# Attention feeding a mixture of experts: fewer filling products, one write of the last unit's rows, an earlier table, another wait on SyncE, two splits moved

## The chip, the cores and the metric

The kernel runs on one core of a Trainium2 chip. The time is that of the device in microseconds (us), measured over whole executions. The engines are called by the profile's names: PE (TensorE, matrix products), PEld (its weight loads), DVE (VectorE), ACT (ScalarE), POOL (GpSimd) and SP (SyncE, which only issues transfers).

## The reference

The kernel computes attention and gives its output, without leaving the chip, to a layer of experts:

```python
# q, k, v: (4 batches, 12 heads, 448 rows, 64)
scores = cap * np.tanh(scale * (q @ k.T) / cap)        # cap = 30
attn = softmax(scores)
x = (attn @ v) -> rows of 4 * 448 = 1792 tokens, 768 wide
logits = (x / |x|) @ (emb / |emb|).T / tau             # 8 experts
expert = argmax(logits); gate = softmax(logits)[expert]
for e in range(8):                                     # w1[e]: 768 x 1024, w2[e]: 1024 x 768
    h = np.maximum(x[expert == e] @ w1[e], 0)
    out[expert == e] = gate * (h @ w2[e])
```

Which expert a token goes to is known only when its attention is done. How many tokens each expert has is data, so the kernel gathers its tiles of 128 rows by a table of row numbers that it computes itself.

## The kernel before

**Precision.** The products of the experts use two half-precision parts of each factor (high and low), as three products: high by high, low by high, high by low. So a weight that has come from memory is split: ACT writes the high part (L238) and DVE the low part (L239). The rows of a tile, x_tile, are transposed on PE (L226), and split in the same way into xh (ACT, L229) and xl (DVE, L230).

**Start.** PE first runs filling products (`warm`, L293) on constants; one tiny product (`cap_t`, L292) that spreads the value cap over all lanes stands in the middle of them, after the eighth of sixteen. Then the attention's scores begin. The tables of expert embeddings are normalised on DVE, transposed on PE, and multiplied into v (`embed_v`), so that the attention gives the logits as extra columns of x.

**Attention.** `attention_bounded` runs 12 units of two head pairs each, in 7 steps: scores on PE, tanh (L839) and exp (L843) on ACT, and four steps later the product with v (L878). `take` divides the sums of a head pair by their denominators on DVE (L891 to L905) and puts them into the buffer xsb, and `write_rows` (L463) has SP write these columns to x_dram in memory: once after each of a unit's two takes, 144 columns wide. For the last batch each is a pair of transfers, for the row blocks "a" and "c". A take of the last unit writes the buffer from which the earlier write reads.

**First expert.** The expert with the most tokens in the first batches is chosen early; its weights are loaded and split during the attention. Its first tile's up products follow the last unit (`do_up`); between them the squares of x (L443), the one-hot choice of experts (`oh_all`, L485) and the ranks of the last batch (L509) are worked out.

**Table and second tile.** The second tile of the first expert runs through `tile_body`: two halves of up products (`up`, L248, 72 products each in 6 calls), `relu` (ACT L259, DVE L260 `hl`), then eight calls of `down` (L687); between the sixth and seventh it transposes the next tile's x. `hook(n)` runs what a table lists for place n: hooks1 (L1333) puts `slots` at 0, and at 12, which is behind both halves and their relus, `fill_table` (L1263), `positions` and `start_loads2` (L1313). `fill_table` multiplies 16 times on PE (`tabp`, L1266), writes the table of row numbers on DVE (L1267), has POOL gather the first tile by it (L207: indices to idx_in, then an indirect transfer into xg), scales the gathered rows into x_tile (`scale_x`: POOL first copies the gate out of xg, L213, then the expert's number to pos_l, then multiplies, L216) and gathers the next tile into the same xg. `start_loads2` has SP read pos_l, which comes behind the gather on POOL, and then issue the loads of the second expert's weights that are still missing: three of w1 (w1r, L1316) and four of w2 (w2r). So these loads stay behind the first gather. The splits of the first three w1 loads stand at places 12, 13 and 14.

**Chain.** `chain(0)` runs the remaining tiles of the first expert. Its first tile splits the other seven loads of the second expert: `step` takes them from a list, with the counts of `pace`: FIRST0 = (1, 1, 1) means one ahead of each half of the ups, and one ahead of each of the first six downs while any are left. With 2 + 6 places all seven are split before the transposes of the next tile (and before `along_transpose`, L1404 to L1407, which does the same for the tails of other experts). The orders of PE, ACT, DVE and POOL are those in which the code is written (`manual_schedule`).

Of the kernel before, what the change touches and what calls it, by code (L numbers as in the profile page):

```python
# [33 lines left out]
I32 = mybir.dt.int32  # L34
# [42 lines left out]

WARM, EARLY = 4, 16

# [5 lines left out]

FIRST, FIRST0 = (4, 4, 1), (1, 1, 1)

# [8 lines left out]
def attention_moe(ctx: ExitStack, tc: tile.TileContext, q, k, v, cap, emb, tau, w1, w2, qk_pairs, v_pairs, vt_pairs, out):  # L96
# [114 lines left out]

    def scale_x(then=None):
        nc.gpsimd.tensor_copy(gate_s, xg[:, GATE : GATE + 1])  # L213
        if then:
            then()
        nc.gpsimd.tensor_tensor(  # L216
            x_tile.rearrange("p (h d) -> p h d", d=DH), heads(xg[:, :SCALE]),
            xg[:, SCALE : SCALE + 1].unsqueeze(2).to_broadcast([P, H, DH]), op=ALU.mult,
        )

    def transpose_x():
# [65 lines left out]
    with tc.tile_pool(name="ps_w", bufs=1, space=PSUM) as ps_w:  # L287
        warm = ps_w.tile([P, 512], F32, name="warm")
        for n in range(EARLY):
            if n == EARLY // 2:  # L290
                t = ps_t.tile([P, 512], F32, tag="t", name="cap_t")
                nc.tensor.matmul(t[:, 0:1], ones_1, cap_b[0:1], start=True, stop=True)  # L292
            nc.tensor.matmul(warm, ones16, a_all[:, 0:4, :], start=True, stop=True)  # L293
# [26 lines left out]
    with ExitStack() as actx:  # L320
# [339 lines left out]
        def tile_body(p, idx, nxt, todo=(), pace=FIRST, hooks=(), hidden=None, first=False, holds=True):  # L660
# [13 lines left out]
            def step(n):  # L674
                for _ in range(min(n, len(todo))):
                    f, *a = todo.pop(0)
                    f(*a)
# [27 lines left out]
            for f in range(6):  # L705
                hook(2 * DC + f)
                step(pace[2])
                down(f)
# [94 lines left out]
        def attention_bounded(apool, ps_s):  # L803
# [145 lines left out]
            with tc.manual_schedule():  # L949
# [21 lines left out]
                for g0 in range(0, last_step + LAG, 2):  # L971
# [8 lines left out]
                    for j in (g0 - LAG, g0 + 1 - LAG):  # L980
                        if j < 0:
                            continue
                        values(j)
                        i, u = divmod(j, STEPS)
                        if u == REST:
                            take(2 * i)
                            behind += 1.1 if i < NH - 3 else 1.4
                            b, n = divmod(i, NP // 2)
                            write_rows(b, 4 * n * HW, (4 * n + 2) * HW, "ac" if b == last else "a")
                        if u == STEPS - 1:  # L990
                            take(2 * i + 1)
                            behind += 1.1 if i < NH - 3 else 1.4
                            b, n = divmod(i, NP // 2)
                            if b < last:
                                odd_heads(b, n)
                            write_rows(b, (4 * n + 2) * HW, 4 * (n + 1) * HW, "ac" if b == last else "a")
                            if n == NP // 2 - 1 and b < last:
                                after(b)
# [198 lines left out]
    pos_i = work.tile([1, 2, E], I32, name="pos_i")  # L1197
    pos_l = work.tile([1, 1], I32, name="pos_l")
    table = work.tile([P, NTAB], I32, name="table")
# [63 lines left out]
    def fill_table(start):  # L1263
# [4 lines left out]
        gather(col(start))  # L1268
        scale_x(lambda: nc.gpsimd.tensor_copy(pos_l, pos_e[:, 1:2]))
        gather(col(start + 1))  # L1270
# [42 lines left out]
    def start_loads2():  # L1313
        e = nc.values_load(pos_l, engines=(ET.SP,), min_val=0, max_val=E - 1)
        for i in range(SOON, N1):
            nc.sync.dma_start(raw1[i], w1_part(e, i))  # L1316
        for f in range(N2):
            nc.sync.dma_start(raw2[f], w2_part(e, f))

    ends = {}  # L1320

    def load_ends(p):
# [14 lines left out]
        ],  # L1337
        12: [lambda: fill_table(start), positions, start_loads2],
        13: [lambda: along_gather()],
# [464 lines left out]
```

## Time and profile before

| What | us |
|---|---|
| median of three timed runs | 463.24 (463.09 to 463.65) |
| profiled execution, whole | 460.33 |
| its span (first to last instruction) | 458.7 |
| PE busy | 427.9 (93%) |
| ACT busy | 280.7 (61%) |
| DVE busy | 258.0 (56%) |
| POOL busy | 103.5 (23%) |
| PE clock granted over the span, mean | 0.981 of full |

The span is 1.63 shorter than the profiled execution's time, and that execution is 2.9 shorter than the timed median. A share of busy time is an average over all stages. In the rows below, a line gives the start in us from the span's begin, the length in us of the group of instructions that follow one another, the engine, the source line and the operation; in brackets stands how long the engine was idle before it, and what ended that. PEclk is the clock that PE was granted: 1.00 is 2.4 GHz, 0.50 is 1.2 GHz.

### The profile page before, as it was taken

The numbers are of one execution on the slowest core, as the hardware profiler recorded it, in microseconds if no ns is written. First come the engines' busy times: TensorE is split into PE (matmuls) and PEld (weight loads), VectorE is DVE, ScalarE is ACT, GpSimd is POOL, SyncE is SP. The second block draws the span as 40 slices with busy tenths as digits, with TensorE's granted clock in tenths as the row PEclk, the third lists the DMA queues.
The fourth block names the chain that finished last, engine by engine and source line by source line (L and its number), as shares of the span: only waits on it lengthen the run. The fifth ranks groups of instructions, "written<-read, shape, count | busy, mean of one in ns | idle before, by whom it ended". The sixth has DMA issues, their size and how long they took to land. (4 is left out here: it accounts for less than half of the span.)

```text
span 458.7 us, 16438 instructions
## 1 busy us (share of the span) xinstructions
PE 427.9 (93%) x6981; PEld 345.9 (75%) x6982; DVE 258.0 (56%) x679; ACT 280.7 (61%) x341; POOL 103.5 (23%) x177
## 2 busy tenths in 40 slices
PE   8999999999999998897979999999999999999971
PEld 3787888887887887584868968878869788687750
DVE  5254268588987897984591128521117711287841
ACT  4998999999998993524651237512228612477840
POOL 4000000100010302115691322312312313214430
PEclk9899999999999999998989999999999999999996
DMA  6754766866687672045982229912207832199110
GB/s 247 233 147 131 230 183 215 270 185 246 209 249 243 175 231 66 6 174 168 364 350 74 74 93 400 400 74 74 73 5 271 281 156 74 24 322 305 62 42 11
DMA packets 37260, 81.80 MB, mean 178 GB/s; under 512 B 8319, under 2 KB 18203, under 8 KB 37156
## 3 DMA queue, kind: packets, MB, share of 16 engines
q1 hardware_dynamic: 33794, 67.35, 43.2%
q0 software_dynamic: 2720, 13.05, 8.8%
q8 instruction: 63, 1.03, 0.9%
q14 instruction: 41, 0.34, 0.2%
q10 hardware_dynamic: 642, 0.03, 0.1%
HBM read 68.37 MB, written 12.21 MB: 176 GB/s over the span
## 5 line engine op out<-in xcount | busy, mean ns | idle before, releaser
L878 PEld LDWEIGHTS v<-vb,prob 128*64 128x64 f32 (+1 forms) x2688 | 79.8, 137 | 17.4 <-issue 16.1
L878 PE MATMUL v<-vb,prob 128*64 128x73 f32 (+1 forms) x2688 | 87.1, 230 | 1.6 <-issue 1.6
L839 ACT ACTIVATE prob<-s,icap 128x896 f32<-128x896 f32 x84 | 80.2, 998 | 11.2 <-PE s L829 9.8
L843 ACT ACTIVATE prob<-prob,cap_b 128x1792 f32<-128x1792 f32 (+1 forms) x47 | 76.8, 1633 | 1.5
L248 PEld LDWEIGHTS <-h 128*128 128x128 f16 x960 | 74.8, 99 | 3.1 <-ACTq L1180 1.3
L248 PE MATMUL h<-xl,h 128*128 128x128 f16 x432 | 74.2, 221 | 1.7 <-DVE xl L230 1.7
L248 PE MATMUL h<-xh,h 128*128 128x128 f16 x432 | 74.2, 221 | 1.6 <-ACTq L1180 0.9
L248 PE MATMUL h<-xh,l 128*128 128x128 f16 x432 | 74.1, 221 | 0.0
L260 DVE SCALAR_TENSOR_TENSOR hl<-h,hh 128x512 f16<-128x512 f32 (+1 forms) x19 | 12.9, 677 | 69.1 <-ACT hh L259 69.1
L248 PEld LDWEIGHTS <-l 128*128 128x128 f16 x480 | 47.4, 99 | 1.9 <-issue 1.9
L259 ACT ACTIVATE hh<-h 128x512 f16<-128x512 f32 (+1 forms) x19 | 11.1, 586 | 59.0 <-PE h L248 55.6
L239 DVE SCALAR_TENSOR_TENSOR l<-w1r,by_pos,h 128x1024 f16<-128x1024 f32 x30 | 37.1, 1281 | 16.3 <-ACT h L238 16.3
L687 PEld LDWEIGHTS <-hh 128*128 128x128 f16 x320 | 31.1, 99 | 19.2 <-issue 1.1
L1449 PE MATMUL h<-xh,h 128*128 128x160 f16 x192 | 39.9, 233 | 3.0 <-ACT room L314 1.9
L229 ACT CAST xh<-xt 128x384 f16<-128x384 f32 x30 | 13.0, 480 | 44.8 <-PE xt L226 44.8
L1449 PE MATMUL h<-xh,l 128*128 128x160 f16 x192 | 39.9, 233 | 0.0
L1449 PE MATMUL h<-xl,h 128*128 128x160 f16 x192 | 39.9, 233 | 0.0
L687 PE MATMUL v<-h,hl 128*128 128x384 f16 x160 | 39.4, 329 | 0.5 <-DVE hl L260 0.5
L687 PE MATMUL v<-h,hh 128*128 128x384 f16 x160 | 39.5, 329 | 0.4 <-DVE left L1299 0.4
L687 PE MATMUL v<-l,hh 128*128 128x384 f16 x160 | 39.6, 329 | 0.1
L239 DVE SCALAR_TENSOR_TENSOR l<-w2r,by_pos,h 128x1536 f16<-128x1536 f32 x20 | 35.5, 1814 | 3.8 <-ACT h L238 3.8
L230 DVE TENSOR_TENSOR xl<-xt,xh 128x384 f16<-128x384 f32 x30 | 15.4, 552 | 39.4 <-ACT xh L229 39.2
(310 smaller groups left out, 814.5 us busy)
## 6 DMA issues: line engine op xcount, KB each, us to landing
w1r<-in_moe_w_dram SPq DMA_DIRECT2D x30, 512.0 KB, 6.3
w2r<-in_moe_w_dram SPq DMA_DIRECT2D x20, 768.0 KB, 7.6
qkb<-in_qk_pairs_dram SPq DMA_DIRECT2D x11, 896.0 KB, 6.2
vb<-in_v_pairs_dram SPq DMA_DIRECT2D x12, 511.0 KB, 5.5
x_dram<-xsb SPq DMA_DIRECT2D x27, 216.0 KB, 3.9
vt<-in_vt_pairs_dram SPq DMA_DIRECT2D x12, 448.0 KB, 4.7
ring<-in_moe_w_dram SPq DMA_DIRECT2D x6, 512.0 KB, 5.7
ring<-in_moe_w_dram SPq DMA_DIRECT2D x5, 384.0 KB, 4.6
```

What stands on the lines that cost most here:

```text
L229: nc.scalar.copy(hi, t)
L230: nc.vector.tensor_tensor(lo, t, hi, op=ALU.subtract)
L239: nc.vector.scalar_tensor_tensor(out=lo, in0=raw, scalar=scale, in1=hi, op0=ALU.mult, op1=ALU.subtract, accum_out=acc)
L248: nc.tensor.matmul(hp[:, f, :], l[j][:, c], x[:, j, :P], start=j == 0 and f == 0 and n == 0, stop=j == DC - 1 and f == 3 and n == 2, skip_ ...
L259: nc.scalar.activation(hh, hp, AF.Relu)
L260: nc.vector.scalar_tensor_tensor(out=hl, in0=hp, scalar=0.0, in1=hh, op0=ALU.max, op1=ALU.subtract, accum_out=acc[:, h : h + 1])
L687: nc.tensor.matmul(y, hidden[h][l][:, c, :], w2p[p % 2][w][f // 2][:, f % 2, m * 384 : (m + 1) * 384], start=f == 0 and n == 0, stop=f == ...
L839: nc.scalar.activation(o, sp[:, :, :S], AF.Tanh, scale=icap)
L843: nc.scalar.activation(o, o, AF.Exp, scale=cap_b)
L878: nc.tensor.matmul(psum_v[2 * i + n][h * DH : (h + 1) * DH, m * VW : (m + 1) * VW], pt[rows, s, c : c + DH], vb[rows, k, s, :], start=m == ...
L1449: nc.tensor.matmul(o, w1p[p % 2][l][j][:, c], x[:, j, :], start=j == 0 and f == fs[0] and m == 0, stop=j == DC - 1 and f == fs[-1] and m == 2,
```

## The change

1. EARLY falls from 16 to 8 filling products, and cap_t stands after the third.
2. FIRST and FIRST0 get other last numbers, and `tile_body` takes one split ahead of each of the first pace[2] downs instead of pace[2] ahead of each of six. For FIRST0 = (1, 1, 3) five splits stand ahead of the transposes, and two come at the end of the tile.
3. The last unit writes its rows once, 288 columns after its second take, instead of 144 after each take.
4. `fill_table` moves from place 12 to 11, which is ahead of the last call of `up` and of the second relu.
5. pos_l and its copy go. SP issues a transfer of one element, `landed<-xg`, which waits for the gather, and then the loads by the register that it already has. The next gather overwrites xg and so waits for `landed`.
6. `scale_x` multiplies first and copies the gate after it, everywhere.

```diff
-WARM, EARLY = 4, 16
+WARM, EARLY = 4, 8
-FIRST, FIRST0 = (4, 4, 1), (1, 1, 1)
+FIRST, FIRST0 = (4, 4, 6), (1, 1, 3)
...
-    def scale_x(then=None):
-        nc.gpsimd.tensor_copy(gate_s, xg[:, GATE : GATE + 1])
-        if then:
-            then()
+    def scale_x():
         nc.gpsimd.tensor_tensor(
             x_tile.rearrange("p (h d) -> p h d", d=DH), heads(xg[:, :SCALE]),
             xg[:, SCALE : SCALE + 1].unsqueeze(2).to_broadcast([P, H, DH]), op=ALU.mult,
         )
+        nc.gpsimd.tensor_copy(gate_s, xg[:, GATE : GATE + 1])
...
         for n in range(EARLY):
-            if n == EARLY // 2:
+            if n == 3:
...
             for f in range(6):
                 hook(2 * DC + f)
-                step(pace[2])
+                step(f < pace[2])
                 down(f)
...
-                            write_rows(b, 4 * n * HW, (4 * n + 2) * HW, "ac" if b == last else "a")
+                            if i < NH - 1:
+                                write_rows(b, 4 * n * HW, (4 * n + 2) * HW, "ac" if b == last else "a")
...
-                            write_rows(b, (4 * n + 2) * HW, 4 * (n + 1) * HW, "ac" if b == last else "a")
+                            c0 = (4 * n + 2 * (i < NH - 1)) * HW
+                            write_rows(b, c0, 4 * (n + 1) * HW, "ac" if b == last else "a")
...
         gather(col(start))
-        scale_x(lambda: nc.gpsimd.tensor_copy(pos_l, pos_e[:, 1:2]))
+        nc.sync.dma_start(landed, xg[0:1, 0:1])
+        scale_x()
         gather(col(start + 1))
...
     def start_loads2():
-        e = nc.values_load(pos_l, engines=(ET.SP,), min_val=0, max_val=E - 1)
         for i in range(SOON, N1):
-            nc.sync.dma_start(raw1[i], w1_part(e, i))
+            load1(1, i)
         for f in range(N2):
-            nc.sync.dma_start(raw2[f], w2_part(e, f))
+            load2(1, f)
...
-        12: [lambda: fill_table(start), positions, start_loads2],
+        11: [lambda: fill_table(start)],
+        12: [positions, start_loads2],
```

How the instructions of two engines stand at the places where they move (the numbers behind a name are those of buffers). DVE in the second tile of the first expert, from the comparison that `slots` ends with (bm) to the first row of `positions` (val); hl0 and hl1 are the low parts of the two relus. Before:

```order
L1255 TENSOR_TENSOR bm_4981<-iota_t_80,slot_4968 128x640
L260 SCALAR_TENSOR_TENSOR hl0_5056,acc_4854<-h0_4852,hh0_5055 128x512
L260 SCALAR_TENSOR_TENSOR hl1_5132,acc_4854<-h1_4853,hh1_5131 128x512
L702 TENSOR_TENSOR sums_132<-sums_132,acc_4854 128x2
L1267 TENSOR_SCALAR table_4820<-tabp_5137 128x40
L1274 COPY val_4816<-scale_w_104 128x16
```

The same stretch of DVE in the changed kernel (line numbers are those of its code):

```order
L1255 TENSOR_TENSOR bm_4971<-iota_t_80,slot_4958 128x640
L258 SCALAR_TENSOR_TENSOR hl0_5046,acc_4844<-h0_4842,hh0_5045 128x512
L1267 TENSOR_SCALAR table_4810<-tabp_5109 128x40
L258 SCALAR_TENSOR_TENSOR hl1_5151,acc_4844<-h1_4843,hh1_5150 128x512
L700 TENSOR_TENSOR sums_132<-sums_132,acc_4844 128x2
L1275 COPY val_4806<-scale_w_104 128x16
```

The table's row has moved ahead of the second relu's low part. The second place is ACT at the end of chain(0)'s first tile: h2 with a number and w2r are the high part and the raw form of a piece of w2, xt are the transposed rows of the next tile, along_h those of the tails. Before:

```order
L238 ACTIVATE h210_4798<-w2r0_4812,by_pos_4817 128x1536
L238 ACTIVATE h211_4799<-w2r1_4813,by_pos_4817 128x1536
L238 ACTIVATE h212_4800<-w2r2_4814,by_pos_4817 128x1536
L238 ACTIVATE h213_4801<-w2r3_4815,by_pos_4817 128x1536
L229 CAST xh_136<-xt0_5553 128x3x128
L229 CAST xh_136<-xt1_5559 128x3x128
L231 COPY gates2_138<-gates2_138 128x1
L1406 CAST along_h_4824<-s0_5585 128x384
L1406 CAST along_h_4824<-h2_5591 128x384
L1414 COPY xh_136<-along_h_4824 128x6x32
```

The same stretch of ACT in the changed kernel:

```order
L236 ACTIVATE h210_4788<-w2r0_4802,by_pos_4807 128x1536
L236 ACTIVATE h211_4789<-w2r1_4803,by_pos_4807 128x1536
L227 CAST xh_136<-xt0_5529 128x3x128
L227 CAST xh_136<-xt1_5535 128x3x128
L229 COPY gates2_138<-gates2_138 128x1
L1407 CAST along_h_4814<-s0_5561 128x384
L1407 CAST along_h_4814<-h2_5567 128x384
L1415 COPY xh_136<-along_h_4814 128x6x32
L236 ACTIVATE h212_4790<-w2r2_4804,by_pos_4807 128x1536
L236 ACTIVATE h213_4791<-w2r3_4805,by_pos_4807 128x1536
```

The last two splits of w2 now stand behind the casts of the transposed rows; DVE's halves of them move in the same way.

## Rows read from the trace of the kernel before

**Rows 1.** Windows by stage: us, busy (count) of PE PEld DVE ACT POOL, PEclk, DMA, GB/s
```profile
14.80:18.10 3.30, 3.30 (x40) 2.62 (x38) 1.33 (x2) 3.23 (x5) 0.13 (x1) 0.50 0.58 134
213.00:216.10 3.10, 3.10 (x12) 2.17 (x13) 1.11 (x2) 1.05 (x3) 2.43 (x7) 0.50 0.92 318
237.10:240.00 2.90, 2.90 (x28) 2.90 (x28) 2.76 (x4) 0.53 (x2) 2.60 (x8) 0.50 0.65 264
```

**Rows 2.** Timeline of the start: start, length, engine, line, operation, out<-in, [idle <-releaser]
```profile
5.04 1.90 PE L293 MATMUL warm<-a_all,ones 128*128 128x512 f16 x8
...
9.47 0.59 DVE L799 CAST hi<-qkb 128x832 fp32r<-128x832 f32 x1 [1.88 <-DMA qkb<-in_qk_pairs_dram]
...
13.29 0.99 PE L856 MATMUL ve<-en_t,vt 128*64 128x16 f32 x28 [0.52 <-DVE en_t L349]
```

**Rows 3.** Timeline, end of attention
```profile
179.78 0.61 DVE L892 TENSOR_TENSOR xsb<-v,inv 128x432 f32<-128x432 f32 x1 [2.28 <-DMA x_dram<-xsb]
...
180.42 0.84 ACT L443 ACTIVATE junk<-xsb 128x768 f32<-128x768 f32 x1 [1.81 <-DVE xsb L892]
...
182.94 0.18 PE L509 MATMUL rp<-oh_all,upper 128*128 128x32 f16 x1 [2.28 <-DVE oh_all L485]
...
184.52 1.11 ACT L238 ACTIVATE h<-ring,first_s 128x384 f16<-128x384 f32 x2
```

**Rows 4.** Timeline from the ups to the gathered tile, and landings of xg's gathers
```profile
195.14 0.23 PE L248 MATMUL h<-xh,h 128*128 128x128 f16 x1 [0.93 <-ACTq L1180]
...
203.19 0.56 PE L1266 MATMUL tabp<-bm,a_all 128*128 128x40 f16 x16
...
204.83 0.19 DVE L1267 TENSOR_SCALAR table<-tabp 128x40 int32<-128x40 f32 x1
...
206.32 1.06 POOL L207 DMA_INDIRECT xg<-x_dram,idx_in  x1 [0.95 <-DMA w1r<-in_moe_w_dram]
...
207.63 1.28 DVE L239 SCALAR_TENSOR_TENSOR l<-w1r,by_pos,h 128x1024 f16<-128x1024 f32 x1 [0.42 <-ACT h L238]
...
210.05 1.28 DVE L239 SCALAR_TENSOR_TENSOR l<-w1r,by_pos,h 128x1024 f16<-128x1024 f32 x1
...
210.27 1.11 POOL L213 COPY gates<-xg 128x1 f32<-128x1 f32 x1 [2.89 <-DMA xg<-x_dram,idx_in]
...
211.47 1.46 POOL L216 TENSOR_TENSOR x_tile<-xg 128x768 f32<-128x768 f32 x1
...
212.28 1.40 SPq L1316 DMA_DIRECT2D w1r<-in_moe_w_dram  x3
...
212.98 1.54 PE L226 MATMUL xt<-ident,x_tile 128*128 128x128 f32 x6 [2.84 <-POOL x_tile L216]
...
213.32 1.05 POOL L207 DMA_INDIRECT xg<-x_dram,idx_in  x1 [0.27 <-POOL idx_in L206]
...
217.17 0.22 PE L248 MATMUL h<-xh,h 128*128 128x128 f16 x1
...
DMA to landing us min/median/max: 3.9/7.8/8.1
...
231.06 0.82 PE L226 MATMUL xt<-ident,x_tile 128*128 128x128 f32 x6
```

**Rows 5.** Page, part 2: GB/s in 40 equal slices of the span
```profile
GB/s 247 233 147 131 230 183 215 270 185 246 209 249 243 175 231 66 6 174 168 364 350 74 74 93 400 400 74 74 73 5 271 281 156 74 24 322 305 62 42 11
```

**Rows 6.** Timeline around the second idle time of PE
```profile
233.12 1.58 ACT L238 ACTIVATE h<-w2r,by_pos 128x1536 f16<-128x1536 f32 x1 [1.49 <-DMA w2r<-in_moe_w_dram]
...
233.99 0.49 PE L1404 MATMUL h<-ident,room 128*128 128x128 f32 x3
...
234.60 0.84 ACT L229 CAST xh<-xt 128x384 f16<-128x384 f32 x2
...
236.47 1.02 DVE L230 TENSOR_TENSOR xl<-xt,xh 128x384 f16<-128x384 f32 x2
...
237.08 0.26 PE L248 MATMUL h<-xl,h 128*128 128x128 f16 x1 [1.75 <-DVE xl L230]
```

More of the change, by code (lines that the diff above doesn't have):

```diff
@@ L1197, in attention_moe @@
     pos_i = work.tile([1, 2, E], I32, name="pos_i")
-    pos_l = work.tile([1, 1], I32, name="pos_l")
+    landed = work.tile([1, 1], F32, name="landed")
     table = work.tile([P, NTAB], I32, name="table")
```

## Prediction, written before the changed kernel ran

> **What bounds the kernel now.** Three views, in this order. The page's busy shares say TensorE (PE) is busy 93% of the span, so time is to be had only where PE stands idle or runs at half clock. The windows by stage give the granted clock, and with it three stretches at 0.50, that is 1.2 instead of 2.4 GHz [rows 1]: one in the attention's first steps, one around 213 to 216 and one around 237 to 240. A stretch of 3.30 at half clock gives 1.65 of full-clock work, so each costs some 1.5 us beside the idle time ahead of it. Then the timeline around these places, with what ended each idle time, leads to four chains that the change touches: the fillers and the first scores [rows 2], the end of attention [rows 3], the table, the gather and the tile that waits for it [rows 4], and the first tile after that, whose xl comes late [rows 6]. All times are of the one profiled execution: 460.33 us, of which the span is 458.7. The three timed runs have a median of 463.24, 2.9 above it. Differences are worked out in the profiled execution and taken off the median.
>
> **Fillers (16 to 8, cap_t behind the third).** Eight fillers took 1.90 [rows 2], so PE can be free of them up to 1.9 us sooner. That need not bring anything: the second half of qk was split at 9.47 only after a DMA wait of 1.88, and the embeddings for v (13.29) waited for en_t from VectorE (DVE) [rows 2], and neither depends on PE. Scores that come earlier meet the same DMA. Against it: PE waits in these steps too (0.52 ahead of 13.29 [rows 2]), and the clock fell at 14.8 [rows 1]; with eight products fewer it may fall sooner or for longer, and one more stretch like it costs 1.65. Bounds -1.9 and +1.65; I take +0.4, near zero because the next link is a transfer, and on the losing side because only the clock reacts to PE alone. The Trainium skill, "TensorE: Matmul & The Clock Gate", section "What's actually happening", speaks against this edit: throttled is the clock's default, and activity releases it. The trace agrees in so far as the clock fell at 14.8 although sixteen fillers had run; by that rule alone the sum would have +1.65 here.
>
> **Last unit's rows.** The last take's multiplication, L892 at 179.78, stood 2.28 waiting for the row transfer that reads the same buffer [rows 3]. The change issues that transfer after the take, and by the order DVE then waits only for its own engine. The wait goes. Behind it in one chain stand the squares on ScalarE (ACT; wait 1.81) and the one-hot that PE's rank products wait for (wait 2.28), then the next weight split at 184.52 [rows 3]. What is late next is ACT, whose wait was the shorter, so I take 1.8, with bounds 0 (ACT's splits keep the old pace) and 2.28. The wider transfer starts with the end of the last take, earlier than the old second half did; its cover is the 20 us until the gather reads the rows.
>
> **Table ahead of relu.** The sixteen tabp products (0.56) ran at 203.19, so done at 203.75, but DVE wrote the table only at 204.83: relu's hl stood ahead of it [rows 4]. In the change tabp stands ahead of the last 12 up products. 144 of these took 8.05 (195.14 to 203.19), one 0.056 and 12 of them 0.67. So tabp ends at 203.08, and the table, with nothing ahead of it, starts near 203.2, 1.6 sooner. PE does the same work in another order: nothing there. With the old distance of 1.49 from table to gather, the gather goes out at 204.7 instead of 206.32 and lands after the least 3.9 at 208.6 instead of 210.2 [rows 4]. The relu and the positions behind it come 0.3 later; the down products after the ups cover that.
>
> On GpSimd (POOL) the order is now x_tile (1.46) ahead of the copy of the gate, and the copy for pos_l is gone. The copy took 1.11 because it ran beside DVE's L239 (210.05 to 211.33) [rows 4] and ended with it. If x_tile starts between the first two of the three splits, which follow one another from 207.63, some 0.3 later than now, it runs from 209.2 to 210.7 (case A); if it has to let one more of 1.28 pass, to 211.9 (case B). It ended at 212.93 before. The Trainium skill, "SBUF — State Buffer", section "🔬 SBUF: two separate sides", has the port pair of DVE and GpSimd as an exclusive lock, kept for a whole instruction. The copy of 1.11 agrees; by that rule the case is B if DVE gets the pair first, and nothing in it lets POOL in after the first split, where case A needs that.
>
> PE's wait for x_tile was 2.84, so it was free at 210.14 [rows 4]. From there in case A: transposes at 210.75, 0.82 at full clock [the row of 231.06 in rows 4], then twelve down products of 384 columns, three times 0.056 each, 2.0: 213.6; xl, which waits for the last split on DVE, is ready at 213.75. The next tile's first product was at 217.17, so the gain is 3.4, 1.5 of it the half clock of 213.0 to 216.1 [rows 1]. Case B: 211.9 + 0.82 + 2.0 = 214.7, gain 2.5. Bounds 0 and 4.0; I take A.
>
> **The small transfer instead of pos_l.** SyncE (SP) waited for POOL's copy before the loads (212.28). Now it waits for the landing itself, at 208.6, issues `landed`, and loads. Queued behind that wait on SP are only those loads, so they start some 3 us sooner. Two things are added: POOL's second gather waits for `landed` to arrive, and up to seven loads are issued ahead of it instead of about two. A price for so small a transfer no row has; the first gather's 3.9 is the nearest, and 0 is the lower end. `landed` at 212.5 is about when x_tile and gate copy are done: 0 on the path. The gather landed in 7.8 (median, under load [rows 4]), from 213 at 221, and its tile's transposes ran at 231.06, so it has some 7 us of cover after the 1.46 of x_tile and PE's 3.4.
>
> **Two splits moved.** ACT's last w2 split began at 233.12, after a wait of 1.49 for its transfer, and held xh until 234.60; DVE's share held xl until 236.47; PE had ended its transposes at 234.48 and waited, apart from one product, until 237.08 [rows 6]: 2.6 lost. Then came 2.90 at 0.50, 1.45 lost [rows 1]. The change puts the last two of seven splits behind the transposes' copies: ACT is free when xt comes, and DVE has two splits less ahead of xl, which then is ready about when PE needs it. Gain 2.6 + 1.45, with a little for the third wait: 4.2. Bounds 0 and 4.2. The deferred splits must be done before the next tile's first down, some 8 us of up products (8.05 for 144) later; two of 1.58 on ACT and their halves on DVE fit into that, but relu's hl stands behind them, and without this cover they would cost up to 1.5.
>
> **Sum.** +0.4 - 1.8 - 3.4 - 4.2 = -9.0. The profiled execution goes from 460.33 to 451.3, the median from 463.24 to 454.3.
>
> **Rivals.**
> First, x_tile no earlier. For it: the trace puts POOL's wait before the first gather down to a weight transfer (w1r, 0.95 [rows 4]) and not to the table; and the three splits in a row may keep POOL out until 211.6, so that x_tile ends at 213.1. Against it: the gather's index needs nothing of a weight transfer, and the gate copy was done when the split ended beside which it began; no row shows POOL passed over at an earlier end of a split. Then the table's term is 0: 463.24 + 0.4 - 1.8 - 4.2 = 457.6. Chance 0.12.
> Second, the late xl stays. For it: the wait of 1.49 for w2r shows that this stage is also fed late, and the loads' speed is the same. Against it: the two splits that wait are those moved, and the loads start 3 us sooner. Its term is 0: 463.24 + 0.4 - 1.8 - 3.4 = 458.4. Chance 0.08.
> Third, the other side: the second gather starves. With seven loads ahead of it instead of two and the transfers at 364 and 350 GB/s in the slices to 240.8 [rows 5], it could land only when that stretch ends, 240.8 less 3: 237.8, and x_tile 1.5 later at 239.3. PE needs it at 231.06 less 3.4, at 227.7. The price is 11.6, and 1.5 for the clock: 454.3 + 13.1 = 467.4. It begins to cost at a landing after 226.2, 13 after the issue, and makes the kernel slower from about 235. Against it: 7.8 was reached while two loads were ahead and others behind, and seven loads (three of 128x1024 and four of 128x1536 floats) hold 4.7 MB, 13 us at 350 GB/s, which bring the landing near 222 to 226. Chance 0.05.
> Fourth, the change of clock at the start alone differs: a whole stretch more (+1.65 instead of +0.4) gives 455.5, inside the range of the forecast.
>
> **How the numbers follow.** Forecast 0.75, the first rival 0.12, the second 0.08, the third 0.05. The forecast's own range is 451.9 (rows term 2.28, no loss at the start, 1.5 of scatter between the profiled and the timed runs) to 456.5 (case B and a clock stretch). With the first two rivals the range is 451.5 to 459.0, and about 2 in 10 stay outside. A measurement of this kernel can tell some 0.2% from no change, 0.93 us. Faster than that are the first three cases; both rivals together with a stretch at the start would give about 462, and the third rival lies on the other side: faster 0.91, same 0.03, slower 0.06.
>
> **What the profile of the changed kernel shows if this holds.** The take L892's wait of 2.28 is gone and the first ups are 1.8 sooner. The table stands right behind tabp, the gather goes out 9.6 instead of 11.2 after the first up product (195.14 to 206.32 before), x_tile ends within 2.5 of its landing, and PE waits under 1 us for it; no stretch at 0.50 near 213. xl is ready when PE ends the transposes, and the stretch near 237 is at full clock. The forecast is wrong if x_tile still ends after the third L239, if PE waits for a deferred split's w2 in the down products, or if the tile after next begins with a wait for xg.

## The result

The changed kernel took 450.81 us as the median of six executions (449.94 to 453.01), against 463.16 for six of the kernel before; the ratio is 0.9747 with a 95% interval of 0.9718 to 0.9776. The forecast was 454.3 with a range of 451.5 to 459.0, so the measured median lies 0.7 below the range. The direction held, and so did three of the four terms; one had the wrong sign. A second series of the same kernel had a median of 454.27, against 462.66 for the kernel before (ratio 0.981, 0.975 to 0.987), which is inside the range. Medians here are over all executions; the ratios, and medians of series taken together, leave out executions more than 1.5% above the fastest of their kernel. In the one profiled execution the kernel took 449.94, its span 448.2 against 458.7: 10.5 less, where the sum had 9.0.

### The profile after

First the clock, in windows of the changed kernel (us, busy time and count of PE, PEld, DVE, ACT and POOL, granted clock, DMA share, GB/s), at the places that answer to [rows 1]:

```profile
13.90:17.10 3.20, 3.20 (x34) 2.51 (x32) 1.45 (x2) 3.13 (x5) 0.13 (x1) 0.50 0.76 151
207.40:210.10 2.70, 2.67 (x19) 1.88 (x20) 2.70 (x6) 0.95 (x3) 2.43 (x3) 1.00 0.96 346
227.30:230.30 3.00, 3.00 (x55) 2.99 (x54) 1.57 (x4) 2.97 (x5) 2.52 (x10) 1.00 1.02 419
```

The two stretches at half clock behind the waits are gone; the one at the start is still there. Then the timeline of the changed kernel's start, which answers to [rows 2]:

```profile
3.69 1.89 PE L291 MATMUL warm<-a_all,ones 128*128 128x512 f16 x4
...
6.18 0.57 PE L827 MATMUL s<-lo,hi 64*128 64x448 f32 x2
...
7.14 1.01 ACT L837 ACTIVATE prob<-s,icap 128x896 f32<-128x896 f32 x1 [3.50 <-PE s L827]
...
8.69 0.59 DVE L797 CAST hi<-qkb 128x832 fp32r<-128x832 f32 x1 [1.97 <-DMA qkb<-in_qk_pairs_dram]
```

The first scores and the first tanh of the kernel before:

```profile
7.31 0.37 PE L829 MATMUL s<-lo,hi 64*128 64x448 f32 x2
...
7.93 1.01 ACT L839 ACTIVATE prob<-s,icap 128x896 f32<-128x896 f32 x1 [4.28 <-PE s L829]
```

The first tanh starts at 7.14 instead of 7.93, though the wait for qk's second half is there as before. A pair of score products takes 0.37 in the kernel before and 0.57 here, so the first scores now run at the lower of the two clock levels; from 6.93 on a pair takes 0.37 to 0.38 here too. (The windows can't tell this: the record of the granted clock begins with its first change, here at 6.9.) The end of attention, for [rows 3]:

```profile
176.35 0.61 DVE L890 TENSOR_TENSOR xsb<-v,inv 128x432 f32<-128x432 f32 x1
...
177.33 0.83 ACT L441 ACTIVATE junk<-xsb 128x768 f32<-128x768 f32 x1
...
191.91 0.23 PE L246 MATMUL h<-xh,h 128*128 128x128 f16 x1 [1.10 <-DVE a_all L548]
```

The take has no wait, nor have the squares. The table, the gather and the tile behind it, for [rows 4]:

```profile
199.30 0.56 PE L1266 MATMUL tabp<-bm,a_all 128*128 128x40 f16 x16
...
199.90 0.20 DVE L1267 TENSOR_SCALAR table<-tabp 128x40 int32<-128x40 f32 x1 [0.52 <-PE tabp L1266]
...
201.40 1.06 POOL L207 DMA_INDIRECT xg<-x_dram,idx_in  x1 [0.98 <-DMA w1r<-in_moe_w_dram]
...
204.77 1.28 DVE L237 SCALAR_TENSOR_TENSOR l<-w1r,by_pos,h 128x1024 f16<-128x1024 f32 x1 [0.42 <-ACT h L236]
...
205.37 0.73 SPq L1269 DMA_DIRECT2D landed<-xg  x1
205.49 1.89 POOL L213 TENSOR_TENSOR x_tile<-xg 128x768 f32<-128x768 f32 x1 [3.03 <-DMA xg<-x_dram,idx_in]
...
205.98 2.48 DVE L237 SCALAR_TENSOR_TENSOR l<-w1r,by_pos,h 128x1024 f16<-128x1024 f32 x1
...
207.43 0.88 PE L224 MATMUL xt<-ident,x_tile 128*128 128x128 f32 x6
...
209.98 1.05 POOL L207 DMA_INDIRECT xg<-x_dram,idx_in  x1 [0.27 <-POOL idx_in L206]
...
210.10 0.22 PE L246 MATMUL h<-xh,h 128*128 128x128 f16 x1
...
217.38 1.46 POOL L213 TENSOR_TENSOR x_tile<-xg 128x768 f32<-128x768 f32 x1 [4.17 <-DMA xg<-x_dram,idx_in]
```

The table stands 0.6 behind the start of tabp instead of 1.6. x_tile was issued beside the first split, took 1.89 and ended at 207.38, and the second split, 2.48 instead of 1.28, waited for it: POOL got its turn between the first and the second (case A). The second gather landed 7.4 after its issue, with seven loads ahead of it: it did not starve. Last the tile behind, for [rows 6]:

```profile
224.56 0.86 ACT L227 CAST xh<-xt 128x384 f16<-128x384 f32 x2 [1.43 <-PE xt L224]
...
225.18 1.01 DVE L228 TENSOR_TENSOR xl<-xt,xh 128x384 f16<-128x384 f32 x2
...
227.40 0.22 PE L246 MATMUL h<-xl,h 128*128 128x128 f16 x1
...
228.37 3.04 ACT L236 ACTIVATE h<-w2r,by_pos 128x1536 f16<-128x1536 f32 x2
```

xl is done at 226.2, 1.2 ahead of the product that reads it. The deferred splits run under the next tile's up products.

### The profile page after: what moved, and what is told of

The parts are those of the page before. It is cut to its first block, busy times and chain, and to the rows that moved or that the text cites. A ratio compares the mean times of both kernels' runs of the same rounds, so it can differ in the third digit from the quotient of the medians.

```text
span 448.2 us, 16416 instructions
## 1 busy us (share of the span) xinstructions
PE 423.5 (95%) x6973; PEld 342.9 (77%) x6974; DVE 257.1 (57%) x679; ACT 280.3 (63%) x341; POOL 103.9 (23%) x176
## 5 line engine op out<-in xcount | busy, mean ns | idle before, releaser
L246 PE MATMUL h<-xh,h 128*128 128x128 f16 x432 | 72.9, 219 | 1.1 <-DVE a_all L548 1.1
L246 PE MATMUL h<-xl,h 128*128 128x128 f16 x432 | 72.9, 219 | 0.0
L246 PE MATMUL h<-xh,l 128*128 128x128 f16 x432 | 72.9, 219 | 0.0
L237 DVE SCALAR_TENSOR_TENSOR l<-w1r,by_pos,h 128x1024 f16<-128x1024 f32 x30 | 38.3, 1321 | 14.7 <-ACT h L236 14.6
L213 POOL TENSOR_TENSOR x_tile<-xg 128x768 f32<-128x768 f32 x15 | 22.4, 1490 | 79.8 <-PE xt L224 68.4
```

Source lines behind the costliest of these rows:

```text
L213: nc.gpsimd.tensor_tensor(x_tile.rearrange("p (h d) -> p h d", d=DH), heads(xg[:, :SCALE]), xg[:, SCALE : SCALE + 1].unsqueeze(2).to_broad ...
L237: nc.vector.scalar_tensor_tensor(out=lo, in0=raw, scalar=scale, in1=hi, op0=ALU.mult, op1=ALU.subtract, accum_out=acc)
L246: nc.tensor.matmul(hp[:, f, :], l[j][:, c], x[:, j, :P], start=j == 0 and f == 0 and n == 0, stop=j == DC - 1 and f == 3 and n == 2, skip_ ...
```

## The experiments

Every execution varies, so the stages were compared by distances between fixed events of each profile: the start of the tenth tanh (A), from there to the last tanh (B), to the second tile's first up product (C), to the third tile's first up product (D), to the first small product of a later tile, `s<-h,hh` (E), and to the end of the span (F). Each number is the difference of two starts in that run's timeline.

| Kernel | A | B | C | D | E | F | median, us | ratio to before, 95% interval |
|---|---|---|---|---|---|---|---|---|
| before | 25.66 | 144.07 | 25.41 | 22.03 | 71.41 | 170.07 | 463.16 | |
| changed | 24.87 | 143.82 | 23.22 | 18.19 | 67.46 | 170.62 | 450.81 | 0.972 to 0.978 |
| changed, again | 24.37 | 146.45 | 23.32 | 18.17 | 67.48 | 169.72 | 454.27 | 0.975 to 0.987 |
| sixteen fillers | 25.36 | 144.42 | 23.53 | 19.35 | 67.92 | 170.81 | 454.13 | 0.981 to 0.988 |
| sixteen, cap_t third | 25.74 | 145.38 | 22.56 | 18.18 | 67.97 | 170.23 | 455.35 | 0.983 to 0.994 |
| 32 fillers | 29.14 | 147.60 | 23.02 | 18.23 | 67.83 | 173.19 | 458.07 | 0.980 to 0.999 |
| four fillers | 24.37 | 148.69 | 22.97 | 18.17 | 67.41 | 170.50 | 449.14 | 0.963 to 0.980 |
| four fillers, again | 23.62 | 144.76 | 23.26 | 18.17 | 68.10 | 170.64 | 449.60 | 0.968 to 0.977 |
| four, table at 10 | 23.63 | 144.49 | 23.08 | 18.34 | 67.41 | 170.23 | 449.64 | 0.970 to 0.980 |
| two row writes | 23.84 | 148.37 | 23.61 | 18.18 | 67.50 | 171.99 | 454.18 | 0.979 to 0.985 |
| two writes, again | 23.85 | 146.10 | 25.87 | 18.17 | 67.54 | 171.25 | 454.06 | 0.976 to 0.987 |
| seven splits ahead | 25.32 | 145.77 | 23.21 | 18.18 | 71.94 | 170.74 | 457.18 | 0.987 to 0.994 |
| table behind relus | 25.82 | 146.11 | 23.14 | 21.91 | 67.41 | 170.30 | 456.39 | 0.980 to 0.996 |
| gate first, pos_l | 24.99 | 146.50 | 23.16 | 19.51 | 67.48 | 170.25 | 453.71 | 0.974 to 0.992 |

Each row's columns come from one profile. C, D and E move with the edits that touch them, with one large exception (D of the first kernel with sixteen fillers, 19.35, explained below). A moves without an edit too: with the same eight fillers it runs from 23.8 to 25.8. B and F, which no edit touches, run from 143.8 to 148.7 and from 169.7 to 173.2. A median of a few executions is therefore known only to some 2 to 4 us (the changed kernel's two series differ by 3.5), and the verdicts below rest on the columns.

### The start: fillers and cap_t

The first kernel is the changed one with both put back:

```diff
-WARM, EARLY = 4, 8
+WARM, EARLY = 4, 16
-            if n == 3:
+            if n == EARLY // 2:
```

> The changed kernel with its fillers put back: sixteen, and cap_t behind the eighth; all else as changed. First theory: the fillers stand in the path of the first scores, and what the first tanh loses is carried through the whole attention. Then the first tanh starts near 7.9 instead of 7.14, the tenth near 25.7 instead of 24.87, the second tile's first up product near 192.9 instead of 191.9, and the span is about 449.2 instead of 448.2. Rival: the attention follows the landing of the second half of qk, which came 0.8 sooner by chance in the one profiled execution. Then the tenth tanh follows that landing and not the first tanh, and the span can be anywhere within 0.5 of 448.2. By the prediction's own estimate (fillers gone cost 0.4 through the clock) the span would be 447.8.

The first tanh started at 8.68, the tenth at 25.36: 0.5 later than in the changed kernel's first profile, 1.0 later than in its second. The second kernel has EARLY = 16 and leaves cap_t behind the third.

> The changed kernel with sixteen fillers again, but cap_t left behind the third. It parts the two halves of the edit. If the number of fillers counts, the first tanh starts at 7.9 or later (all sixteen still stand ahead of the first scores) and the tenth near 25.7, as with the full undo. If the place of cap_t counts (the scale of the tanh hangs on it), the first tanh stays near 7.2 and the tenth near 24.9. If neither counts, the tenth tanh follows the landing of the second half of qk alone.

The first tanh came at 7.93 and the tenth at 25.74, just as before the change. So the place of cap_t gives nothing while the fillers stand behind it; their number counts. (In every trace of a kernel that has cap_t behind the third filler, it runs behind the fourth.) The next has EARLY = 32:

> The changed kernel with 32 fillers, cap_t still behind the third. The dose shows how much cover the fillers have. One costs 0.24 at full clock, so the first scores come 24 x 0.24 = 5.7 later than with 8. If the fillers stand in the path at any dose, the tenth tanh comes 5.7 later than the 24.87 with 8, near 30.5; if the transfers of the second half of qk (landing near 9) give them cover, the first 2 or so are hidden, and it comes near 28.5. If only the clock hung on the fillers, more of them would leave no stretch at half clock in the first 25, and give back up to 1.65 of this.

The first tanh of the kernel with 32 fillers:

```profile
12.47 1.01 ACT L837 ACTIVATE prob<-s,icap 128x896 f32<-128x896 f32 x1 [8.82 <-PE s L827]
```

The first tanh is 5.33 later than with eight fillers and the tenth 4.3, between the two expectations (28.5 and 30.5), though qk's second half was split at 8.29, sooner than in any profile with eight or sixteen. This profile has no stretch at half clock near 14; against the three with eight fillers that have none either (24.37, 23.84, 23.85) the tenth is 5.1 later. So the transfer on which the forecast leaned hides little of the 5.7 that 24 fillers take. What stands behind the first tanh is ACT itself, which a window of the changed kernel shows without a pause (columns as above; the fourth number with a count is ACT's):

```profile
8.00:12.00 4.00, 2.98 (x24) 1.23 (x21) 2.55 (x6) 3.93 (x5) 0.29 (x1) 1.00 1.03 417
12.00:16.00 4.00, 3.49 (x44) 2.76 (x46) 2.21 (x5) 3.94 (x5) 0.00 (x0) 0.72 0.90 249
```

In the fourteen profiles the tenth tanh starts 16.7 to 17.1 behind the first where no stretch at half clock lies between, and 17.7 to 18.2 where one does (19.6 in the one with a double stretch). The stretch itself was there in two of three profiles with sixteen fillers, in four of seven with eight, and in none of three with four and of one with 32; so few profiles don't show that the fillers decide it.

What does follow their number is the clock of the first scores. By the lengths of their pairs they ran at the higher level in all three profiles with sixteen fillers, at the lower in six of seven with eight and in all three with four. The exception among the seven is the kernel with the table behind the relus:

```profile
5.61 0.37 PE L827 MATMUL s<-lo,hi 64*128 64x448 f32 x2
...
6.23 1.01 ACT L837 ACTIVATE prob<-s,icap 128x896 f32<-128x896 f32 x1 [2.58 <-PE s L827]
```

Its first tanh is 1.7 sooner than the 7.93 before; in five others of the seven it came at 7.14 to 7.17, in one at 7.70. So eight fillers fewer give 1.7 at the first tanh, and the lower clock of the scores mostly takes 0.9 of it back. The last dose, EARLY = 4:

> The changed kernel with four fillers, cap_t behind the third. If fillers stand in the path all the way, the first tanh starts 0.95 sooner than with 8, near 6.2, and the tenth near 23.9. If the landing of the first half of qk and VectorE's splits of it (low part done at 5.6 in the changed kernel) now decide, both stay within 0.3 of 7.14 and 24.9, and the span within the scatter of the changed kernel's 448.2 to 451.2.

> Four fillers against the changed kernel's eight, on the same chip. In the first profile with four the tenth tanh came at 24.37, against a mean of 24.97 for five profiles with eight and 25.59 for three with sixteen. If fillers cost in the path at this dose too, it comes near 24.4 again and the median is 0.5 below that of the changed kernel; if not, it comes at 24.9 and the medians agree within 0.6.

The tenth tanh came at 24.37 (the scores had waited 2.41 for the scale that is made from cap, and the first tanh started at 7.70) and at 23.62 (first tanh at 6.61). The first score products of the second:

```profile
5.08 0.74 PE L827 MATMUL s<-hi 64*128 64x448 f32 x2 [1.32 <-DVE icap L297]
```

In all three profiles with four fillers PE stood idle for this scale, 1.3 to 2.4: at this dose the fillers are out of the path and VectorE's work holds the scores, as the second theory of the first expectation had it, though not at the times that it named. Means of A: 25.6 with sixteen (three profiles), 24.7 with eight (seven), 23.9 with four (three). Like against like, the step from sixteen to eight stays: 25.7 and 25.1 with one stretch at half clock, 25.4 and 24.0 with none. The step from eight to four does not: with none it is 24.0 and 23.9, and the rest of the 0.8 is the stretch, which by chance or not was missing in all three with four. Nine executions with four fillers have a median of 449.56, eleven with eight 451.26; what part of that the fillers bring the medians can't tell, as B alone varies by more.

### The last unit's rows

The changed kernel with one write after each take again:

```diff
-                            if i < NH - 1:
-                                write_rows(b, 4 * n * HW, (4 * n + 2) * HW, "ac" if b == last else "a")
+                            write_rows(b, 4 * n * HW, (4 * n + 2) * HW, "ac" if b == last else "a")
...
-                            c0 = (4 * n + 2 * (i < NH - 1)) * HW
+                            c0 = (4 * n + 2) * HW
```

> The changed kernel with the last unit's rows written twice again, 144 columns after each take. First theory: the last take waits for the first write to have read its buffer, 2.28 in the kernel before, and the whole wait counts: the squares on ScalarE start near 179.6 instead of 177.33, the second tile's first up product near 194.2 instead of 191.9, the span is about 450.5. By the prediction's estimate ScalarE's shorter wait decides: 1.8, first up product near 193.7, span about 450.0. Rival: another part of the change would have removed this wait anyway (rows landing sooner as the attention starts sooner), and the span stays near 448.2.

> The last unit's rows written twice again, a second look. The first profile had a wait of 0.98 for the first write instead of 2.28 in the kernel before: the write's landing decides, and it changes from one execution to the next. If that is so, the wait is again somewhere between 0.5 and 2.5, and the distance from the last tanh to the second tile's first up product is 23.2 plus about that wait. If 0.98 was a fluke and 2.28 the rule, the wait is 2 or more, and the median is 2 above that of the changed kernel on the same chip.

The last take's multiplication in the first of the two runs:

```profile
180.29 0.61 DVE L890 TENSOR_TENSOR xsb<-v,inv 128x432 f32<-128x432 f32 x1 [0.98 <-DMA x_dram<-xsb]
```

The same in the second, with PE's rank products behind it:

```profile
179.67 0.61 DVE L890 TENSOR_TENSOR xsb<-v,inv 128x432 f32<-128x432 f32 x1 [2.46 <-DMA x_dram<-xsb]
...
182.83 0.18 PE L507 MATMUL rp<-oh_all,upper 128*128 128x32 f16 x1 [1.98 <-DVE oh_all L483]
```

And a window of that run behind the wait:

```profile
184.20:187.50 3.30, 3.30 (x17) 1.79 (x15) 3.20 (x17) 3.30 (x9) 1.40 (x2) 0.50 0.11 9
```

The wait is the write's landing, 0.98 to 2.46 in three profiles, and in one of them a stretch at half clock follows. C has a mean of 25.0 with two writes (three profiles) and 23.1 with one (eleven): the edit is worth 1.8 in the mean, from 0.5 to 2.7. Against the mean with one write C is 2.3 longer for the wait of 2.28, 2.7 for 2.46 and 0.5 for 0.98, so where the wait is long the whole of it counts, and not ScalarE's shorter one. The whole times don't show the edit: in the same series the kernel with two writes took 454.06 and the changed one 454.27.

### The table, and the order on POOL and SP

The changed kernel with the table at place 12:

```diff
-        11: [lambda: fill_table(start)],
-        12: [positions, start_loads2],
+        12: [lambda: fill_table(start), positions, start_loads2],
```

> The changed kernel with the table at place 12 again, behind both relus; the small transfer and the order of scale_x stay changed. First theory: the table's place is worth the 1.6 that it moves the gather. From the second tile's first up product to the table are then 9.7 (before 9.69, changed 7.99), to the end of x_tile 17.1 (changed 15.5), and PE's transposes come 1.6 later with a wait of about 1.6 ahead of them. Rival: POOL is kept out by the three splits on VectorE that follow the gather, so x_tile ends about when the last split lets it, and the table's place alone is worth under 0.5.

Its x_tile and PE's transposes:

```profile
210.41 2.17 POOL L213 TENSOR_TENSOR x_tile<-xg 128x768 f32<-128x768 f32 x1 [3.10 <-DMA xg<-x_dram,idx_in]
...
212.64 1.25 PE L224 MATMUL xt<-ident,x_tile 128*128 128x128 f32 x6 [2.57 <-POOL x_tile L213]
```

The gather landed just behind the start of the third split (209.98), and x_tile ran when that was over: the first theory and its rival are both at work. D lost 3.7, of it 2.0 at the end of x_tile, and the rest through the half clock, which came back from 213.0 to 216.4. The other kernel keeps the table early and puts back the gate's copy ahead of x_tile, and pos_l with the loads behind it:

```diff
-        nc.sync.dma_start(landed, xg[0:1, 0:1])
-        scale_x()
+        scale_x(lambda: nc.gpsimd.tensor_copy(pos_l, pos_e[:, 1:2]))
```

> The changed kernel with the gate's copy ahead of x_tile again, and pos_l in place of the small transfer; the table stays at place 11. First theory: the two copies cost x_tile what they cost before, 1.1 to 1.3 beside a split, and no more: from the second tile's first up product to the end of x_tile 16.6 instead of 15.5, and PE waits about 1 for it. The loads on SyncE go out 1 later than now, which costs nothing, as xl and the splits of w2 have cover. Rival: the late loads bring back the wait of the chain's first tile for w2r, and the distance from the third tile's first up product to the relu of the fourth grows from 22.1 to 24 or more.

POOL in that run:

```profile
208.20 0.62 POOL L213 COPY gates<-xg 128x1 f32<-128x1 f32 x1 [3.02 <-DMA xg<-x_dram,idx_in]
...
208.77 1.25 POOL L1271 COPY pos_l<-pos_e 1x1 int32<-1x1 int32 x1
...
209.99 1.46 POOL L216 TENSOR_TENSOR x_tile<-xg 128x768 f32<-128x768 f32 x1
```

Each copy, a fraction of a microsecond of work, lasted until the split beside it ended, and x_tile came third in turn; PE waited 1.5 and D lost 1.3. E did not move (67.48), so the later loads cost nothing. Undone singly the two edits lose 3.7 and 1.3; together they had gained 3.8. They share one thing, x_tile's place among the splits. (The copies' order and the small transfer were put back together; what each is worth alone was not tested.)

How near the edge that place is, the first kernel with sixteen fillers shows, in which this stage has no edit:

```profile
203.47 1.06 POOL L207 DMA_INDIRECT xg<-x_dram,idx_in  x1 [1.66 <-DMA w1r<-in_moe_w_dram]
...
207.60 2.35 POOL L213 TENSOR_TENSOR x_tile<-xg 128x768 f32<-128x768 f32 x1 [3.07 <-DMA xg<-x_dram,idx_in]
```

The gather went out 10.16 behind the first up product instead of 9.49. x_tile was issued when the first split was over (207.42) and ran behind the second; PE waited 1.36 for it, and D is 1.2 longer: the prediction's case B. What held the gather is not settled; it waits for several transfers, of which the profile names one of weights. In the ten other profiles with the early table and x_tile first, x_tile ends 15.45 to 15.62 behind the first up product; here 16.64.

### The splits

The changed kernel with all seven splits ahead of the transposes:

```diff
-FIRST, FIRST0 = (4, 4, 6), (1, 1, 3)
+FIRST, FIRST0 = (4, 4, 6), (1, 1, 6)
```

> The changed kernel with all seven splits ahead of the transposes again. First theory: xl is late by the two splits, and PE waits as before and falls to half clock behind it: the first tile of the chain ends near its old distance, the relu after it at about 22.4+3.3 us behind the transposes' tile start, the span about 452.2 (4.0 more). Rival: the loads, which now start 3 us sooner relative to the tile, have made the splits early enough in any order, and the span is 448.2 to 449.5.

The chain's first tile in that run:

```profile
229.03 1.58 ACT L236 ACTIVATE h<-w2r,by_pos 128x1536 f16<-128x1536 f32 x1 [1.38 <-DMA w2r<-in_moe_w_dram]
...
231.03 0.22 PE L246 MATMUL h<-xh,h 128*128 128x128 f16 x1 [1.14 <-ACT xh L227]
...
232.39 1.02 DVE L228 TENSOR_TENSOR xl<-xt,xh 128x384 f16<-128x384 f32 x2
...
233.00 0.26 PE L246 MATMUL h<-xl,h 128*128 128x128 f16 x1 [1.75 <-DVE xl L228]
```

The window behind it:

```profile
232.40:235.60 3.20, 2.60 (x25) 2.60 (x25) 2.14 (x7) 1.15 (x3) 2.65 (x12) 0.50 0.94 385
```

All of the stall of [rows 6] is back, the wait for w2r too: the whole stage, its loads included, had moved forward together. E lost 4.5, against 4.0 that the change had gained.

### The changed kernel again, and a further version

> The changed kernel itself, once more, beside the others of this call. If the time forecast was missed only by the scatter between executions (waits of PE during the attention that differ from one execution to the next, 2.5 in all in the profiled execution of before, 5.3 in one of an experiment), its median comes out between 449.9 and 453 again and some executions lie inside the forecast's range of 451.5 to 459.0. If terms were mis-sized, it stays near 450.8 with most executions below 451.5. The tenth tanh starts between 23.8 and 25.8, as in the five profiles with eight fillers so far.

The same kernel took 454.27 this time (449.82 to 457.81), at a ratio of 0.981 (0.975 to 0.987). Both expectations missed it; four of the six executions lie inside the forecast's range. Eleven executions of both series have a median of 451.26. Its columns A, C, D and E agree with the first profile within 0.5; B is 2.6 longer. The further version has EARLY = 4 and the table at place 10.

> A version that could beat both: four fillers, and the table at place 10, one more call of up products (12, 0.67) ahead. The table then waits for the comparison behind slots (bm), which ended at 198.77 against 199.30 for the products of the table in the changed kernel, so up to 0.5 is to be had there, and x_tile ends 0.5 sooner, which PE uses only where it waits for it (0 to 0.3 in the changed kernel's profiles). Expected: the distance from the second tile's first up product to the table is 7.5 instead of 7.99, and the median is within 0.5 of four fillers alone.

The table came 7.53 behind the first up product instead of 7.99, but x_tile, expected 0.5 sooner, ended 15.62 behind it instead of 15.47: it was issued 0.23 sooner and took 2.27 instead of 1.89, as POOL again got its turn only at the end of the first split. D stayed at 18.34. The kernel took 449.64 (448.61 to 453.54), as four fillers alone did. Both have lower medians than the changed kernel's two (450.81, 454.27), though the intervals of the ratios overlap. What the profiles show of it is A, 0.8 shorter in the mean, most of it the missing stretch at half clock; the table brings nothing.

## Why the prediction was wrong, and where it was right

**The step that failed is the first term.** It read "Scores that come earlier meet the same DMA" and took +0.4. The doses show the opposite: from the first tanh on ACT is busy without a pause, so a later first tanh is a later tenth. With sixteen fillers the tenth tanh came at 25.6 in the mean, with eight at 24.7: -0.9 in place of +0.4 (-0.8 between the two first profiles), a miss of 1.2 to 1.3, most of the 1.5 by which the traced sum fell short. The wait of 1.88 for qk was real, but what waited was VectorE, for the second pair; the chain of the first pair ran past it. Two windows of the kernel before would have told:

```profile
8.00:12.00 4.00, 3.27 (x24) 1.13 (x20) 2.43 (x6) 3.94 (x5) 0.38 (x2) 1.00 1.02 414
12.00:16.00 4.00, 3.22 (x46) 2.66 (x46) 2.17 (x6) 3.93 (x5) 0.18 (x1) 0.85 0.87 255
```

ACT is busy 3.94 of the 4.00 from 8 to 12 and 3.93 from 12 to 16. That the 0.8 lasts to the end of attention no single profile can show, as B scatters by more; with PE busy 97 to 100% of the changed kernel's time from 25 to 140 there is little that could hide it.

The same term argued that fewer fillers put the clock at risk, and in this it was right in kind: with eight the first scores ran at half clock in six of seven profiles, with sixteen in none of three. That takes back 0.9 of the 1.7 that the missing fillers give, and so does not turn the sign. The price of +1.65, one more stretch like that of [rows 1], was not paid: that stretch is there or not with eight and with sixteen, and was not seen with four. The rule cited from the Trainium skill, "TensorE: Matmul & The Clock Gate", section "What's actually happening" (throttled by default, activity releases it), agrees with the half clock of the first scores and with the stretch behind idle PE at 120 below.

**The rows: right in the wait; its size varies.** 1.8 was taken; the profiles have 2.2 (before against after) and 1.8 in the mean. That the mean is the forecast is luck: the prediction took ScalarE's wait of 1.81 in place of the take's 2.28, and C shows nearly the whole of a long wait. The size is the write's landing, and so no constant.

**The table and x_tile: right in mechanism and case.** 3.4 forecast, 3.8 measured. The gather went out 9.49 behind the first up product (9.6 forecast), and case A held, here and in nine more of the eleven profiles with the early table and x_tile first; case B came once, where the gather went out 0.7 later. The section "🔬 SBUF: two separate sides" of "SBUF — State Buffer" in the Trainium skill, with its exclusive lock for a whole instruction, was set against case A. The lock is what the trace shows (x_tile 1.89 and the split 2.48, each holding up the other); but in these traces the engine that waits gets the next turn, though a further split is ready. The first rival, x_tile no earlier, is out; its ground, that something other than the table can hold the gather, is not, as the profile with case B has it.

**The small transfer: right.** `landed` cost nothing on the path, the second gather came at 217.38 and PE's next transposes at 224.03. The third rival, the starved gather, is out. The cover of 7 that the prediction gave this gather is 5.2 by its own figures (231.06 less 3.4 and 1.46, from 221), and 5.2 is what the trace has, from x_tile's end at 218.84 to 224.03.

**The splits: right.** 4.2 forecast, 4.0 gained and 4.5 lost on undoing. The second rival is out; the late w2r that spoke for it is real (1.38 with the splits put back), but the two deferred splits no longer pass it on to xl.

**The scatter: too small.** The terms of the traces add to -10.5: A -0.8, B -0.2, C -2.2, D -3.8, E -4.0, F +0.5. That would have given 452.7 from the median of 463.24, which is inside the range: the first term alone does not carry the median out of it. The last 1.9 is in no column: the profiled execution of before was 2.9 below its median, that of after only 0.9 below, and the range allowed 1.5 for this. The range also took 0 as the best case of the start, where the prediction's own bound was -1.9; with that it would have reached down to 450.0. In its second series the changed kernel came out at 454.27, all but on the forecast, and that is luck as well: the traced terms add to 1.5 more than was forecast. The prediction held that 0.93 could be told from no change; two medians of one kernel, 3.5 apart, say otherwise.

## What to carry to other kernels

Before a transfer is taken as cover, ask whose wait it is: here ScalarE was busy without a pause from its first tanh on, and what delayed that tanh was paid nearly in full (5.1 of 5.3 with 32 fillers). A wait on PE can cost twice, once idle and once more at half clock behind it: the one of 2.57 with the late table was followed by such a stretch, and a move of the gather by 1.6 became 3.7 in D, while the waits of 1.50 and 1.36 were not; so two edits need not add up. And compare stages by distances within a profile where whole executions scatter by more than the edit is worth, and look in each profile for what else moved the distance.

## What the runs showed beyond that

Column B moves by waits of PE for which the profile names no releaser. They stand at nearly the same places in most runs (near 38, 106 and 142), last 0.5 to 2.4, and some are followed by a stretch at half clock. The largest, in the first run with four fillers:

```profile
120.01 1.00 PE L876 MATMUL v<-vb,prob 128*64 128x73 f32 x12 [2.39 <-issue]
```

The windows around it:

```profile
112.00:117.60 5.60, 5.60 (x166) 5.04 (x163) 5.50 (x13) 5.24 (x6) 0.00 (x0) 1.00 0.77 210
117.60:120.00 2.40, 0.02 (x2) 0.00 (x0) 2.33 (x7) 1.46 (x1) 0.00 (x0) 0.93 0.39 111
120.00:123.40 3.40, 3.39 (x26) 1.91 (x25) 1.55 (x4) 0.93 (x1) 0.00 (x0) 0.50 0.79 270
```

And the transfers from 115 to 121, by queue:

```profile
q1 hardware_dynamic: 401, 1.18, 61.5%
q8 instruction: 1, 0.02, 1.0%
```

One packet of the queue that the profile calls "instruction" falls into this stretch. The fourteen profiles have forty waits of 0.5 or more without a releaser between 20 and 178, and such a packet ends inside each of them or less than 1 us ahead of it. Chance would give that for about two in five, by the share of the time that the packets' ends cover in this way. But each profile has 32 to 35 of these packets there and one to five of the waits, so most packets hold nothing up. That PE waits for its own instructions is a likely reading; no run tested it.
